# V's weights by contraction blocks in whole rows, and four V sums begun with two of five blocks

## The chip, the cores and the metric

The kernel runs on one core of one Trainium2 chip. The metric is the device time of one execution in microseconds; lower is better. The core has five instruction streams that run beside each other: TensorE (PE, with its weight loads shown as PEld), VectorE (DVE), ScalarE (ACT), GpSimd (POOL) and SyncE (SP). SP issues nearly all of the DMAs here.

## The reference, cut to what matters

The input x is 2048 rows of 640 columns in bf16. A layer norm of x goes into two branches, and their sum with x is the output: attention with 32 heads of 20 columns over a sliding window of 256 rows, and a gated feed-forward part with 1536 hidden columns.

```python
xn = _layernorm(x, axis=-1)                      # (1, 2048, 640)
qkv = xn @ wqkv                                  # wqkv: (640, 3 * 640), columns q | k | v
p = softmax(where(window of 256 keys back, q @ k.T * 20 ** -0.5, -1e9))
A = (p @ v) @ wo
B = (sigmoid(xn @ w_gate) * (xn @ w_up)) @ w_down
return x + A + B
```

## The kernel before

Rows are worked on in four chunks (`c`) of 512, and a chunk in four blocks (`s`) of 128 rows. The contraction over 640 columns is made of five blocks (`d`, `DC` = 5) of 128. `xnT[c]` holds the normed and transposed rows of a chunk, 128 partitions by five blocks by 512 rows; `wqkv` holds all of the q, k and v weights, 128 partitions by five blocks by 1920 columns, of which the last 640 are V's.

The order of every engine's instructions is the order in which the program writes them (`manual_schedule`). Chunk 0 is done by hand at the head; from then on a list of parts (`fill`) is pulled between the steps of the attention at build time, so that TensorE's order is fixed too.

**The head's loads.** SP issues, in this order: rows of x for blocks 0, 1 and 3 (`load_rows`, L157), V's weights for the columns of its first half (`load_v(0)`, L161: all five blocks, 320 columns), the rows of block 2, V's second half (`load_v(1)`), then the q and the k weights (`load_wqkv`, L151), and after those the gate and up weights (`load_gu`, L182).

**Norm and transposes.** Blocks 0 and 3 take their mean and variance on VectorE (`ln_half`, `ln_mv`), blocks 1 and 2 on ScalarE (`mean_act` L620, `root_act` L625 and L626); VectorE writes the normed rows `xn` for all of them (`norm` L273, `norm_act` L630 and L631). `transpose_rows(s, copy, lo, hi)` then turns the five 128 x 128 blocks of a row block on TensorE (`pt`, L280, in the PSUM pool `ps_h`, tag h), and the engine named by `copy` moves them to `xnT` (L281): ScalarE for block 0 in two parts, VectorE for the others.

**V's sums.** `project_v(c, s, hf)` makes one sum: the 128 rows of block `s` by the 320 columns of half `hf`, five matmuls of 128 x 320 (L329) into one PSUM bank `pv`. Eight of them stand in the head. A name such as v10 means block 1, half 0. `copy_v` evacuates a sum in two pieces of 64 rows (`us` 0 and 1) into the tile `v` (L338), by VectorE (`dve`) or ScalarE (`act`). PSUM has eight banks in the head: four under the tag d (pool `ps_d`) and four under the tag h (`ps_h`). A pool gives its banks in turn; two warming sums (`pwarm`, L233) take the first two of d. v30 and v31 stand in h, all other V sums in d.

TensorE's order in the head: the ten warming matmuls, the transposes of blocks 0 and 1, v00, v10, the transposes of block 3, v01, v30, v11, the transposes of block 2, v31, v20, v21, then the ten q and k sums (`proj_block`, L300), whose banks are d again. VectorE evacuates the q sums (L304), ScalarE the k sums (L306); they go by DRAM (`sq`, `sk`, L308) into the layout of the heads (`spread`, L318). After that come the gate and up sums (`pg` L414, `pu` L421) and the attention steps (`ps` L490, `acc` L523).

Of the kernel before, what the change touches and what calls it, by code (L numbers as in the profile page):

```python
# [9 lines left out]
P = 128  # L10
S = 2048
D = 640
# [3 lines left out]
DC = D // P  # L16
FC = F // P
CW = 512
# [4 lines left out]
GH = NG // 2  # L23
VW = DH + 1
VH = 16 * VW + 11
HALF = 320
FS = 768
EPS = 1e-5
# [10 lines left out]
FP32 = mybir.dt.float32  # L39
# [54 lines left out]
def kernel(  # L94
# [11 lines left out]
    nc = tc.nc  # L106
# [4 lines left out]
    def pool(name, bufs, **kw):  # L111
        return ctx.enter_context(tc.tile_pool(name=name, bufs=bufs, **kw))
# [15 lines left out]
    ps_d = pool("ps_d", 4, space=bass.MemoryType.PSUM)  # L128
# [13 lines left out]
    wqkv = const.tile([P, DC, 3 * D], BF16, name="wqkv")  # L142
    wqkv_r = A_wqkv.rearrange("(c p) n -> p c n", p=P)
# [6 lines left out]
    def load_wqkv(part):  # L150
        nc.sync.dma_start(out=wqkv[:, :, part * D:(part + 1) * D],  # L151
                          in_=wqkv_r[:, :, part * D:(part + 1) * D])
# [3 lines left out]
    def load_rows(s, queue):  # L156
        queue.dma_start(out=xc[0][:, s, :], in_=xr[:, s, :])  # L157

    def load_v(hf):
        a = 2 * D + hf * HALF  # L160
        nc.sync.dma_start(out=wqkv[:, :, a:a + HALF], in_=wqkv_r[:, :, a:a + HALF])  # L161

    load_rows(0, nc.sync)
    load_rows(1, nc.sync)
    load_rows(3, nc.sync)
    load_v(0)
    load_rows(2, nc.sync)
    load_v(1)
    load_wqkv(0)
    load_wqkv(1)  # L170

# [58 lines left out]
    for n in (6, 4):  # L230
        ps = ps_d.tile([P, CW], FP32, name="pwarm", tag="d")
# [18 lines left out]
    def ln_half(c, s, a, stats=None):  # L250
        if a == 0:
            stats = lnp.tile([P, 2, nc.vector.BN_STATS_DIM], FP32, name="stats")
        nc.vector.bn_stats(out=stats[:, a, :], in_=xc[c][:, s, a * HALF:(a + 1) * HALF])
        return stats
# [22 lines left out]
    def transpose_rows(s, copy, lo=0, hi=DC):  # L277
        pt = ps_h.tile([P, DC, P], BF16, name="pt", tag="h")
        for d in range(lo, hi):
            nc.tensor.transpose(pt[:, d, :], xns[0, s][:, d * P:(d + 1) * P], ident)  # L280
        copy(out=xnT[0][:, lo:hi, s * P:(s + 1) * P], in_=pt[:, lo:hi, :])  # L281
# [38 lines left out]
    def new_v(c, s):  # L320
        v = vp.tile([P, 2, VH], BF16, name="v")
        vt[c * SBC + s] = v
        nc.gpsimd.memset(v[:, :, 0:16 * VW].rearrange("p k (h d) -> p k h d", d=VW)[:, :, :, DH:VW], 0.5)
        nc.gpsimd.memset(v[:, :, 16 * VW:], 0.0)

    def project_v(c, s, hf, home=ps_d, tag="d"):
        ps = home.tile([P, CW], FP32, name="pv", tag=tag)
        for d in range(DC):
            nc.tensor.matmul(ps[:, 0:HALF], lhsT=xnT[c][:, d, s * P:(s + 1) * P],  # L329
                             rhs=wqkv[:, d, 2 * D + hf * HALF:2 * D + (hf + 1) * HALF],  # L330
                             start=(d == 0), stop=(d == DC - 1))
        return ps

    def copy_v(c, s, hf, ps, copy, us=(0, 1)):

        v = vt[c * SBC + s][hf * U:(hf + 1) * U, :, 0:16 * VW].rearrange("p k (h d) -> p k h d", d=VW)
        for u in us:
            copy(out=v[:, u, :, 0:DH],  # L338
                 in_=ps[u * U:(u + 1) * U, 0:HALF].rearrange("p (h d) -> p h d", d=DH))

    def proj_v(c, s, hf, copy):
        copy_v(c, s, hf, project_v(c, s, hf), copy)
# [265 lines left out]
    def root(mv):  # L608
        r = lnp.tile([P, 1], FP32, name="rstd")
        nc.scalar.activation(out=r, in_=mv[:, 1:2], func=SQRT, bias=eps)  # L610
        return r

    def norm(s, mv, r):
        nc.vector.reciprocal(r, r)
        norm_block(0, s, mv, r)
# [13 lines left out]
    def norm_act(s, xn, neg, r):  # L629
        nc.vector.reciprocal(r, r)  # L630
        nc.vector.tensor_scalar(out=xn, in0=xc[0][:, s, :], scalar1=neg[:, 0:1],  # L631
                                scalar2=r[:, 0:1], op0=ADD, op1=MULT)
        xns[0, s] = xn
# [4 lines left out]
    act, dve = nc.scalar.copy, nc.vector.tensor_copy  # L638
# [8 lines left out]
    norm_act(1, xn1, neg1, r1)  # L647
    mv3 = ln_mv(ln_half(0, 3, 1, stats3))
    transpose_rows(1, dve)
    v00 = project_v(0, 0, 0)  # L650
    r3 = root(mv3)
    xn2, neg2 = mean_act(2)
    r2 = root_act(2, xn2, neg2)
    norm(3, mv3, r3)
    v10 = project_v(0, 1, 0)
    copy_v(0, 0, 0, v00, dve, (0,))
    transpose_rows(3, dve)
    v01 = project_v(0, 0, 1)
    norm_act(2, xn2, neg2, r2)
    copy_v(0, 0, 0, v00, act, (1,))  # L660
    copy_v(0, 1, 0, v10, act)
    v30 = project_v(0, 3, 0, ps_h, "h")
    copy_v(0, 0, 1, v01, act)
    v11 = project_v(0, 1, 1)
    copy_v(0, 3, 0, v30, act)
    transpose_rows(2, dve)
    v31 = project_v(0, 3, 1, ps_h, "h")
    copy_v(0, 1, 1, v11, dve)
    copy_v(0, 3, 1, v31, act)
    proj_v(0, 2, 0, dve)  # L670
    proj_v(0, 2, 1, act)
# [75 lines left out]
    c = NCH - 1  # L747
# [62 lines left out]
```

## Time and profile before

| What | Value |
|---|---|
| Median of 3 timed runs | 309.93 us (309.67 to 310.23) |
| Profiled execution, its own time | 309.64 us |
| Its span, first to last instruction | 307.9 us |
| Granted TensorE clock | 1.000 |
| Busy of the span: PE, ACT, DVE, POOL | 98%, 64%, 56%, 55% |
| V matmuls of the head (L329) | 40, started from 7.0 to 13.1 us |
| First q matmul (L300) | 13.20 us |
| DMA in the first 13.2 us | 3.70 MB, mean 281 GB/s |

Times inside the profile are microseconds from the start of its span. A row of an order of time gives the start, the length, the engine, the line, what was written from what, and in brackets how long the engine had been idle and what released it. Matmuls overlap in their pipeline and their ends are modelled: the distance from start to start tells what one costs.

### The profile page before, as it was taken

How to read it: one execution, taken by the hardware profiler on the slowest of the kernel's cores; microseconds unless marked ns; L12 is line 12 of the kernel's file. 1: busy time of each engine (PE TensorE's matmuls, PEld its weight loads, DVE VectorE, ACT ScalarE, POOL GpSimd, SP SyncE). 2: the span in 40 equal slices, each digit the busy share in tenths (PEclk: the TensorE clock that was granted, in tenths of full speed). 3: DMA queues.
4: the chain of work that ended last, by engine and by line, in shares of the span. 5: the costliest groups of instructions: out<-in, count | busy, mean ns of one | idle time of the engine just before them, and what ended most of it. 6: DMA issues, size and time to landing. Idle time of an engine off the chain costs nothing.

```text
span 307.9 us, 9937 instructions
## 1 busy us (share of the span) xinstructions
PE 300.4 (98%) x4276; PEld 167.7 (54%) x4311; DVE 171.2 (56%) x339; ACT 198.4 (64%) x197; POOL 168.7 (55%) x308
## 2 busy tenths in 40 slices
PE   7999999999999999999999999999999999999995
PEld 3654444555657654554457654554546664444774
DVE  4633667648698364487946164383734536363523
ACT  6923877698854649888674547878585547688000
POOL 6000686687874828576672728457372937566000
PEclk9999999999999999999999999999999999999999
DMA  7997986984709363630015312650000200000202
GB/s 220 366 319 237 333 161 199 351 228 144 234 2 127 69 179 124 189 109 2 3 24 87 87 57 87 209 162 0 3 2 2 86 27 21 2 2 6 84 21 67
DMA packets 40460, 35.68 MB, mean 116 GB/s; under 512 B 10560, under 2 KB 39872, under 8 KB 40384
## 3 DMA queue, kind: packets, MB, share of 16 engines
q1 hardware_dynamic: 39552, 34.27, 38.6%
q10 hardware_dynamic: 864, 0.77, 0.8%
q8 instruction: 34, 0.56, 0.8%
q14 instruction: 10, 0.08, 0.1%
HBM read 23.63 MB, written 10.26 MB: 110 GB/s over the span
## 4 chain that ended last, share of the span: by engine, by line
PE 96%; issue 1%; DMA 1%; ACT 1%; DVE 0%; SPq 0%
PE y L435 18%; PE pu L421 17%; PE pg L414 17%; PE pqk L300 14%; PE ps L490 9%; PE pv L329 7%; PE y L442 7%; PE acc L523 6%; DMA xc<-in_A_x_dram 1%; PE pt L280 0%; ACT xn L620 0%; ACT xn L625 0%; DVE xn L631 0%; SPq L157 0%; ACT rstd L626 0%
## 5 line engine op out<-in xcount | busy, mean ns | idle before, releaser
L507 POOL TENSOR_SCALAR_AFFINE_SELECT pT<-pT 64x512 bf16<-64x512 bf16 (+1 forms) x256 | 157.1, 614 | 109.1 <-ACT pT L496 96.6
L496 ACT ACTIVATE pT<-ps 128x2048 bf16<-128x2048 f32 (+1 forms) x76 | 141.0, 1855 | 59.8 <-PE ps L490 57.9
L425 DVE SCALAR_TENSOR_TENSOR h<-th,pu 128x512 bf16<-128x512 f32 x48 | 32.8, 683 | 51.4 <-PE pu L421 44.9
L421 PE MATMUL pu<-xnT,wu 128*128 128x512 bf16 x228 | 59.0, 380 | 0.7 <-issue 0.2
L414 PE MATMUL pg<-xnT,wg 128*128 128x512 bf16 x226 | 58.5, 380 | 0.9 <-issue 0.3
L435 PE MATMUL y<-wd,h 128*128 128x320 bf16 (+2 forms) x396 | 56.8, 295 | 0.0
L300 PE MATMUL pqk<-xnT,wqkv 128*128 128x512 bf16 x191 | 45.4, 381 | 0.6 <-issue 0.2
L435 PEld LDWEIGHTS <-h 128*128 128x128 bf16 x396 | 36.7, 98 | 15.9 <-issue 1.8
L417 ACT ACTIVATE th<-pg 128x512 f32<-128x512 f32 x48 | 28.6, 595 | 15.5 <-PE pg L414 15.4
L414 PEld LDWEIGHTS <-wg 128*128 128x128 bf16 x240 | 22.3, 98 | 25.8 <-issue 2.0
L421 PEld LDWEIGHTS <-wu 128*128 128x128 bf16 x240 | 22.0, 98 | 25.5 <-issue 2.0
L300 PEld LDWEIGHTS <-wqkv 128*128 128x128 bf16 x200 | 22.5, 119 | 18.7 <-issue 1.4
L535 DVE STREAM_TRANSPOSE t<-acc 128x512 f32<-128x512 f32 x32 | 21.1, 696 | 20.1 <-PE acc L523 20.1
L490 PE MATMUL ps<-qT,kT 20*64 20x320 bf16 (+4 forms) x1440 | 32.1, 260 | 0.0
L490 PEld LDWEIGHTS <-kT 20*64 20x64 bf16 x1440 | 15.4, 103 | 24.9 <-issue 21.8
L446 DVE SCALAR_TENSOR_TENSOR rows<-y,rows 128x320 bf16<-128x320 f32 x30 | 14.4, 488 | 25.9 <-PE y L442 25.7
L547 DVE TENSOR_TENSOR on<-t,rec 128x320 bf16<-128x320 f32 (+4 forms) x48 | 27.8, 579 | 1.1
L329 PE MATMUL pv<-wqkv,xnT 128*128 128x320 bf16 x160 | 25.8, 300 | 0.0
L442 PE MATMUL y<-wo,oc 128*128 128x320 bf16 (+2 forms) x165 | 24.2, 295 | 0.0
L338 DVE CAST v<-pv 64x320 bf16<-64x320 f32 x29 | 14.1, 486 | 12.5 <-PE pv L329 12.3
L523 PE MATMUL acc<-pT,v 64*32 64x320 bf16 (+4 forms) x1440 | 19.7, 253 | 0.0
L523 PEld LDWEIGHTS <-v 64*32 64x32 bf16 x1440 | 16.2, 91 | 5.8 <-ACT pT L496 1.7
(48 smaller groups left out, 157.3 us busy)
## 6 DMA issues: line engine op xcount, KB each, us to landing
qT<-sq SPq DMA_DIRECT2D x16, 256.0 KB
kT<-sk SPq DMA_DIRECT2D x16, 256.0 KB
sq<-st SPq DMA_DIRECT2D x20, 128.0 KB
sk<-st SPq DMA_DIRECT2D x20, 128.0 KB
out_dram<-rows SPq DMA_DIRECT2D x15, 160.0 KB
wg<-in_B_w_gate_dram SPq DMA_DIRECT2D x4, 480.0 KB
wu<-in_B_w_up_dram SPq DMA_DIRECT2D x4, 480.0 KB
xc<-in_A_x_dram SPq DMA_DIRECT2D x3, 640.0 KB
```

Of the source, the lines that this page charges most:

```text
L300: nc.tensor.matmul(ps, lhsT=wt[:, m, :], rhs=xnT[c][:, d, :], start=(d == 0), stop=(d == DC - 1))
L329: nc.tensor.matmul(ps[:, 0:HALF], lhsT=xnT[c][:, d, s * P:(s + 1) * P], rhs=wqkv[:, d, 2 * D + hf * HALF:2 * D + (hf + 1) * HALF], start=( ...
L414: nc.tensor.matmul(pg, lhsT=part(wg, d, f), rhs=xnT[c][:, d, :], start=(d == 0), stop=(d == DC - 1))
L417: nc.scalar.activation(out=th, in_=pg, func=TANH, scale=0.5)
L421: nc.tensor.matmul(pu, lhsT=part(wu, d, f), rhs=xnT[c][:, d, :], start=(d == 0), stop=(d == DC - 1))
L425: nc.vector.scalar_tensor_tensor(out=h, in0=th, scalar=1.0, in1=pu, op0=ADD, op1=MULT)
L435: nc.tensor.matmul(y[:, 0:cut[1] - cut[0]], lhsT=ht[c, f][:, s * P:(s + 1) * P], rhs=wd[:, f, cut[0]:cut[1]], start=(f == 0), stop=False)
L442: nc.tensor.matmul(y[:, 0:cut[1] - cut[0]], lhsT=oc[c, m][:, s * P:(s + 1) * P], rhs=wo[:, m, cut[0]:cut[1]], start=False, stop=(m == DC - 1))
L490: nc.tensor.matmul(ps[a * U:(a + 1) * U, i, col * U:(col + n) * U], lhsT=qk["k", kc, o // GH][32 * i:32 * i + DH, o % GH + a, kb * U:(kb + ...
L496: nc.scalar.activation(out=pt[:, :, 0:width], in_=ps[:, :, 0:width], func=EXP, scale=SCALE)
L507: nc.gpsimd.affine_select(out=view, in_=view, pattern=[[0, HG], [0, n], [sign, U]], compare_op=GE, fill=0.0, base=base, channel_multiplier ...
L523: nc.tensor.matmul(acc[32 * i:32 * i + 32, q * U:(q + n) * U], lhsT=vt[kb][a * U:(a + 1) * U, u, h * VW:h * VW + 32], rhs=pt[a * U:(a + 1) ...
```

## The change

V's weights are still loaded in two DMAs in the same two places of SP's order, but cut along the contraction: first the blocks 0 and 1 with all 640 columns, then the blocks 2 to 4. A row of a packet is 1280 bytes instead of 640.

Four sums are split. v00 and v01 get their first two matmuls where v00 stood, v10 and v11 theirs where v10 stood. Then come the transposes of block 3, and after them the remaining three matmuls of v00, v01, v10 and v11. Then v30, the transposes of block 2, v31, v20 and v21, as before. `project_v` takes the range of blocks and an open bank for that.

The evacuations keep their engines, but are moved: on VectorE the first piece of v00 comes after the copy of xnT for block 3 instead of ahead of it, and the two pieces of v11 come ahead of the copy of xnT for block 2 instead of behind it. On ScalarE v01 is evacuated ahead of v10.

```diff
+VD = 2
...
-    def load_v(hf):
-        a = 2 * D + hf * HALF
-        nc.sync.dma_start(out=wqkv[:, :, a:a + HALF], in_=wqkv_r[:, :, a:a + HALF])
+    def load_v(lo, hi):
+        nc.sync.dma_start(out=wqkv[:, lo:hi, 2 * D:], in_=wqkv_r[:, lo:hi, 2 * D:])
...
-    load_v(0)
+    load_v(0, VD)
     load_rows(2, nc.sync)
-    load_v(1)
+    load_v(VD, DC)
...
-    def project_v(c, s, hf, home=ps_d, tag="d"):
-        ps = home.tile([P, CW], FP32, name="pv", tag=tag)
-        for d in range(DC):
+    def project_v(c, s, hf, home=ps_d, tag="d", lo=0, hi=DC, ps=None):
+        if ps is None:
+            ps = home.tile([P, CW], FP32, name="pv", tag=tag)
+        for d in range(lo, hi):
...
     transpose_rows(1, dve)
-    v00 = project_v(0, 0, 0)
+    v0 = [project_v(0, 0, hf, hi=VD) for hf in range(2)]
     r3 = root(mv3)
     xn2, neg2 = mean_act(2)
     r2 = root_act(2, xn2, neg2)
     norm(3, mv3, r3)
-    v10 = project_v(0, 1, 0)
-    copy_v(0, 0, 0, v00, dve, (0,))
+    v1 = [project_v(0, 1, hf, hi=VD) for hf in range(2)]
     transpose_rows(3, dve)
-    v01 = project_v(0, 0, 1)
+    for s, vs in enumerate((v0, v1)):
+        for hf in range(2):
+            project_v(0, s, hf, lo=VD, ps=vs[hf])
+    copy_v(0, 0, 0, v0[0], dve, (0,))
+    copy_v(0, 0, 0, v0[0], act, (1,))
+    copy_v(0, 0, 1, v0[1], act)
     norm_act(2, xn2, neg2, r2)
-    copy_v(0, 0, 0, v00, act, (1,))
-    copy_v(0, 1, 0, v10, act)
+    copy_v(0, 1, 0, v1[0], act)
+    copy_v(0, 1, 1, v1[1], dve)
     v30 = project_v(0, 3, 0, ps_h, "h")
-    copy_v(0, 0, 1, v01, act)
-    v11 = project_v(0, 1, 1)
+    transpose_rows(2, dve)
     copy_v(0, 3, 0, v30, act)
-    transpose_rows(2, dve)
     v31 = project_v(0, 3, 1, ps_h, "h")
-    copy_v(0, 1, 1, v11, dve)
     copy_v(0, 3, 1, v31, act)
     proj_v(0, 2, 0, dve)
     proj_v(0, 2, 1, act)
```

## The prediction

> **What bounds the kernel now.** I read the page first, then the busy time by stretches, then the chain of waits through the first 16 us, then TensorE's weight loads and VectorE's instructions in order of time, and last what the DMA engines moved. The page's engine line and its chain by engine come first.
>
> ```profile
> PE 300.4 (98%) x4276; PEld 167.7 (54%) x4311; DVE 171.2 (56%) x339; ACT 198.4 (64%) x197; POOL 168.7 (55%) x308
> ...
> PE 96%; issue 1%; DMA 1%; ACT 1%; DVE 0%; SPq 0%
> ```
>
> TensorE is busy 98% of the span and is 96% of the chain. The kernel's time is therefore the moment at which TensorE gets going plus everything it has to do, plus the few places where it waits. The stretches say where that could still be.
>
> ```profile
> 6.96:13.20 6.24, 6.24 (x54) 4.24 (x52) 4.58 (x13) 5.68 (x15) 0.00 (x0) 1.00 1.07 360
> 13.20:307.90 294.70, 288.83 (x4208) 161.39 (x4240) 163.56 (x319) 188.40 (x173) 163.82 (x286) 1.00 0.38 109
> ```
>
> The columns are the length, then busy time (and instructions) of PE, PE weight loads, DVE, ACT and POOL, the granted clock, the DMA share and GB/s. The first row is the V stage, which the change rewrites; at 13.20 the q projection (L300) begins. After 13.20 the order of TensorE's instructions is the same in both kernels, and in this trace TensorE's only idle entries there are some 0.7 us put down to issue. So I look for the new start of q: a shift of it goes through to the end one to one.
>
> ```profile
> 6.67 0.45 PE pt L280 x5
> 7.13 1.44 PE pv L329 x10
> 8.56 0.28 PE pt L280 x5
> 8.84 2.12 PE pv L329 x15
> 10.96 0.28 PE pt L280 x5
> 11.24 2.12 PE pv L329 x15
> ```
>
> This is the chain inside the V stage (start, length, what): TensorE alone, no DMA. V's weights are not what it waits for. By the landing records, the last piece of V's first column half arrives at 6.75 and of the second at 8.30; the first V matmul starts at 6.96, right behind the transposes of row block 1, and the first that needs the second half at 8.68. Modelled ends make PE look gapless here, so the real gaps must be read from the weight loads (start, length, idle before).
>
> ```profile
> 7.71 0.52 PEld L329 LDWEIGHTS <-xnT 128*128 128x128 bf16 x5 [0.24 <-DVE xnT L281]
> 8.32 0.35 PEld L280 LDWEIGHTS <-xn 128*128 128x128 bf16 x5
> ...
> 9.43 1.20 PEld L329 LDWEIGHTS <-xnT 128*128 128x128 bf16 x10 [0.24 <-DVE xnT L281]
> ...
> 11.82 1.20 PEld L329 LDWEIGHTS <-xnT 128*128 128x128 bf16 x10 [0.24 <-DVE xnT L281]
> ```
>
> Three times TensorE waits for VectorE's copy of a transposed block: for xnT of block 1, 3 and 2. V matmuls start 0.136 us apart and transposes 0.056, so five V matmuls begun at 6.96 are issued by 7.64 and the next starts at 7.71: 0.07 us lost, and 0.07 each at 9.43 and 11.82. The whole V stage loses 0.21 us. That is all that this profile lets a better order gain here.
>
> ```profile
> 8.19 0.48 DVE L338 CAST v<-pv 64x320 bf16<-64x320 f32 x1
> 8.88 0.49 DVE L281 COPY xnT<-pt 128x640 bf16<-128x640 bf16 x1 [0.22 <-PE pt L280]
> 9.62 0.16 DVE L630 RECIPROCAL rstd<-rstd 128x1 f32<-128x1 f32 x1 [0.25 <-ACT rstd L626]
> 9.82 0.45 DVE L631 TENSOR_SCALAR xn<-xc,neg,rstd 128x640 bf16<-128x640 bf16 x1
> 11.28 0.49 DVE L281 COPY xnT<-pt 128x640 bf16<-128x640 bf16 x1 [1.01 <-PE pt L280]
> 11.80 2.02 DVE L338 CAST v<-pv 64x320 bf16<-64x320 f32 x4
> ```
>
> VectorE in order. It stood idle 1.01 us before the copy of xnT for block 2, so that copy began as soon as the transposes were done. The two evacuations of v11 came after it, in the 2.02 us.
>
> **The change, part by part.** *The same work.* TensorE still runs 40 V matmuls and the same transposes, ACT still makes 11 V evacuations and DVE 5; POOL and SP keep their order. Only V's two DMA issues on SP differ in shape, 2 and 3 whole-row blocks for 5 half rows twice, 0.43 us of issue each now; nothing of the V stage waits for a later issue of SP. Cost nothing.
>
> *The loads.* V's 800 KB go in 640 packets of 1280 B for 1280 of 640 B. The trace has both sizes:
>
> ```profile
> 4.50:5.00 0.50, 0.50 (x2) 0.00 (x0) 0.16 (x1) 0.50 (x4) 0.45 (x2) 1.00 1.03 296
> 8.00:10.00 2.00, 2.00 (x20) 1.37 (x18) 1.50 (x5) 1.91 (x6) 0.00 (x0) 1.00 1.06 392
> ```
>
> In 4.50 to 5.00 only 640-byte packets ran (296 GB/s, median 32 ns each), in 8 to 10 only 1280-byte ones beside a few semaphore writes (392 GB/s, 55 ns). By packets the pair shortens by (1280 x 32 - 640 x 55) / 16 = 360 ns; by rates, 819 KB at 296 against 392 GB/s, by 0.68 us. So V is complete at about 7.6 to 7.9 where it was 8.30. The first piece falls from 410 KB to 328 KB, 0.28 us less at 296 GB/s, so 6.47 or earlier where it was 6.75. The needs are 6.96 and (below) 8.61: both hidden, with margins of 0.5 and 0.7 us. Bounds for each: 0 if so, and if the second lands with no gain at all, at 8.30, still 0. The Trainium skill's page "DMA: Bandwidth & Descriptors", section Specifications, puts line rate at 512 B and up, which would make both packet sizes equal and leave V complete at 8.30; the rows above (296 against 392 GB/s) disagree, and by the page's rule the sum stays the same with a margin of 0.3 us in place of 0.7. All later loads come forward by as much, and no matmul after 13.20 waits for one of them, so that gives nothing.
>
> *TensorE up to the third block.* v00 and v01 now take two matmuls each from 6.96: issued by 6.96 + 4 x 0.136 = 7.51. v10 and v11 need xnT of block 1, whose copy ends at 7.65 as before (its chain is untouched), and start at 7.71. The wait is 0.20 where it was 0.07: cost 0.13. Four matmuls end at 8.25. The transposes of block 3 need xn written at 8.27; a weight load followed such an end by 0.05 us at 7.71, 9.43 and 11.82, so they start at 8.33: a new wait of 0.07, which the fifth matmul of v10 covered before. They end at 8.61.
>
> *The rest of the four sums.* Twelve matmuls, 8.61 + 1.63 = 10.24. The wait of 0.07 for xnT of block 3 goes: VectorE makes that copy at about 8.82 to 9.31, straight behind the transposes, and v30 comes only at 10.24. After v30 (five matmuls, 10.92) the transposes of block 2 need xn2. VectorE now evacuates v00 first, from 9.33 to 9.82, so the reciprocal moves from 9.62 to 9.85 and xn2 from 10.27 to about 10.50. Cover 0.42 us; cost nothing. So far the change has lost 0.13 + 0.07 - 0.07 = 0.13 us.
>
> *The moved evacuation.* VectorE's queue now holds both evacuations of v11 ahead of the copy of xnT for block 2. v11's last matmul starts at 10.11 and the sum is readable some 0.32 later (10.66 to 10.98 in the trace), at 10.43; VectorE is free at 10.50, so 10.53 to 11.52 for two of 0.49. The transposes start at 10.92 and can be read at 11.38; the copy then runs 11.55 to 12.04 where it ran 11.28 to 11.77. TensorE finishes v31 at 10.92 + 0.28 + 0.68 = 11.88 and waits for that copy until 12.10: 0.22 in place of 0.07, cost 0.15. If VectorE got v11 0.2 us earlier this would be 0; if its row of three pieces ran 0.1 late, 0.25.
>
> *PSUM homes.* Four sums are open at once and fill all four banks of the d tag. v20 reuses v00's bank, read by 10.04 (ACT), v21 v01's, read by 10.9, the first q block v10's, read by 11.8, and they start at 12.1, 12.8 and 13.5. No wait. ACT's 11 evacuations end near 14.4 as now, and its next use is the k copy at 19.87.
>
> *Sum.* 0.13 + 0.15 = 0.28 on exact clocks 0.27: q starts at about 13.47 for 13.20, and the last instruction moves by as much. The profiled execution took 309.64 us (span 307.9), so it would take 309.91. The three timed runs have the median 309.93 (309.67 to 310.23), 0.29 above the profiled one; on them the forecast is 309.93 + 0.27 = 310.20, a loss of 0.09%. About 0.2%, 0.62 us, is what a measurement of this kernel can tell from no change, so I call it the same, on the slow side. Bounds of the unknown terms: +0.05 (no wait for the moved copy, the new gap at 8.25 closed) to +0.45.
>
> **The rivals.**
>
> *V's second piece decides (slower).* In the old order the second half was first used at 8.68 by one sum, with three more to follow much later; now all twelve middle matmuls, and with them v30 and the transposes of block 2, stand in one queue behind that load. If it lands after 8.61, each microsecond costs one. For it: one of the 16 DMA engines lagged the others by 0.6 us in both V loads (6.09 then 6.75; 7.67 then 8.30), and packets up to 0.77 us long ran near 3.8. Against it: the rates above. It shows as slower from a landing at 8.96; at 9.3 the time is 309.93 + 0.27 + 0.69 = 310.9. Chance 0.2.
>
> *V's first piece was late in ordinary executions (faster).* In the profiled one it was 0.21 us ahead of its use, but the timed median is 0.29 above that execution. If the whole 0.29 were waits for a first half that lands later, the smaller first piece would give it back: 309.93 + 0.27 - 0.29 = 309.9, the same. To be faster by 0.62 the usual wait would have to be 0.9 us, and the fastest timed run is only 0.26 below the median. Chance 0.08, nearly all as unknown variation.
>
> *The new waits do not form.* If VectorE takes v11 earlier than I work out, only the first gaps stay: 310.0. The same class; part of the 0.72.
>
> **How the numbers follow.** The forecast and its neighbours within 0.2% hold 0.72, the late second piece with other knock-on waits 0.20, faster 0.08. The low end, 309.5, is the best timed run less 0.2 (all three old gaps of 0.21 closed); the high end, 311.0, is the second rival value. The likeliest case alone spans 309.9 to 310.5.
>
> **What would show it.** Right: q's first matmul (L300) at about 13.45; weight loads of v10 still at 7.71, of block 3's transposes at 8.33, and of v20 at 12.1 behind VectorE's copy; V's two landings before 6.6 and 8.0; the stretch behind q's start 294.7 us long as now. Wrong: a V matmul that waits for a DMA near 8.6; q's start before 13.2; or a stretch behind q's start that differs by over 0.3 us, which would mean that something after the V stage moved that I took for fixed.

## The result, and the profile after

The changed kernel takes 311.02 us (median of 16 runs, 310.00 to 312.02) where the kernel before takes 309.92 (16 runs, 309.31 to 311.89): ratio 1.0033, 95% interval 1.0017 to 1.0048, a loss of 1.0 us by the ratio. The forecast was a loss of 0.27 us, called the same. The sign was right and the size was not: the median lies at the top end of the stated range (311.0), and the loss is clear of zero and, by its median, over the 0.2% bound. Its profiled execution took 310.83 us, with a span of 309.1 us against 307.9.

The chain by engine on the page after, and then the two stretches cut at the first V matmul and the first q matmul (columns as in the prediction):

```profile
PE 93%; DVE 2%; DMA 2%; issue 1%; SPq 1%; DVEq 0%
```

```profile
6.76:13.55 6.79, 6.55 (x54) 4.28 (x52) 4.68 (x13) 5.75 (x15) 0.00 (x0) 1.00 1.02 346
13.55:309.10 295.55, 288.87 (x4208) 161.32 (x4240) 163.93 (x319) 188.29 (x173) 163.49 (x286) 1.00 0.38 108
```

TensorE's share of the chain fell from 96% to 93%; VectorE (2%) and the DMA of V's weights (2%) are in it now. The V stage is 6.79 us long instead of 6.24, but began 0.20 earlier (6.76 for 6.96, because the rows of block 1 landed at 3.55 instead of 3.76 in this execution), so q starts at 13.55 instead of 13.20: 0.35 of the 1.2 us of span. The other 0.84 stands in the second row, 295.55 for 294.70, which the prediction took for fixed. That is over the 0.3 us that the prediction named as a sign of being wrong.

TensorE's weight loads in the V stage (start, length, idle before and its releaser):

```profile
7.50 0.39 PEld L330 LDWEIGHTS <-xnT 128*128 128x128 bf16 x4 [0.37 <-DVE xnT L281]
8.12 0.28 PEld L280 LDWEIGHTS <-xn 128*128 128x128 bf16 x5 [0.23 <-DVE xn L273]
...
8.78 2.13 PEld L330 LDWEIGHTS <-xnT 128*128 128x128 bf16 x16 [0.32 <-issue]
...
12.17 1.20 PEld L330 LDWEIGHTS <-xnT 128*128 128x128 bf16 x10 [0.31 <-DVE xnT L281]
```

The three waits of the prediction are there: for block 1's xnT (0.20 us by matmul starts), for block 3's xn (0.06) and for block 2's xnT (0.14). The fourth, ahead of 8.78, is not in its sum: the third matmul of v00 could have run at 8.41 and ran at 8.77. The records put the last landing of V's second piece at 8.73. This V matmul that waits for a DMA is another of the prediction's signs of being wrong. VectorE in order shows why the copy of block 2's xnT is later than before:

```profile
8.61 0.49 DVE L281 COPY xnT<-pt 128x640 bf16<-128x640 bf16 x1 [0.55 <-PE pt L280]
...
10.60 1.00 DVE L339 CAST v<-pv 64x320 bf16<-64x320 f32 x2 [0.19 <-PE pv L330]
11.63 0.49 DVE L281 COPY xnT<-pt 128x640 bf16<-128x640 bf16 x1
```

The two evacuations of v11 end at 11.60, and the copy follows them at once, as the prediction had it. Then the list of what TensorE waited for behind q's start has one row that the kernel before did not have (engine, line, releaser, total, times, longest):

```profile
PE y L436 <- DVE h L426: 0.8, 1, 0.8
```

It stands near 156 us, 140 us behind the code that was changed: the down projection of chunk 1 waits for the last `h`. VectorE there, first the kernel before, then the changed one:

```profile
150.78 0.32 DVE L547 TENSOR_TENSOR on<-t,rec 128x192 bf16<-128x192 f32 x1
...
153.20 1.30 DVE L273 TENSOR_SCALAR xn<-xc,mvs,rstds 128x640 bf16<-128x640 bf16 x2
154.42 0.67 DVE L425 SCALAR_TENSOR_TENSOR h<-th,pu 128x512 bf16<-128x512 f32 x1
```

```profile
151.15 0.82 DVE L548 TENSOR_TENSOR on<-t,rec 128x192 bf16<-128x192 f32 x1
...
154.07 1.50 DVE L273 TENSOR_SCALAR xn<-xc,mvs,rstds 128x640 bf16<-128x640 bf16 x2
155.50 0.67 DVE L426 SCALAR_TENSOR_TENSOR h<-th,pu 128x512 bf16<-128x512 f32 x1
```

The same multiply of 192 columns takes 0.82 us instead of 0.32. Everything behind it in VectorE's queue moves by that, and the two norm writes take 1.50 us instead of 1.30, which adds 0.20: `h` ends at 156.17, TensorE's next matmul starts at 156.22. In the kernel before `h` ended at 155.09 and TensorE took it 0.05 us later, so there was no slack at all: the 0.70 us by which VectorE fell back went through to TensorE. TensorE's weight loads for that matmul, first in the kernel before, then in the changed one:

```profile
155.14 0.79 PEld L435 LDWEIGHTS <-h 128*128 128x128 bf16 x7 [0.38 <-DVE h L425]
```

```profile
156.22 0.79 PEld L436 LDWEIGHTS <-h 128*128 128x128 bf16 x7 [1.08 <-DVE h L426]
```

### The profile page after: what moved, and what is told of

It reads as the page before. It is cut to its first block, busy times and chain, and to the rows that moved or that the text cites. A ratio compares the mean times of both kernels' runs of the same rounds, so it can differ in the third digit from the quotient of the medians.

```text
span 309.1 us, 9937 instructions
## 1 busy us (share of the span) xinstructions
PE 300.4 (97%) x4276; PEld 167.5 (54%) x4311; DVE 171.8 (56%) x339; ACT 198.4 (64%) x197; POOL 168.3 (54%) x308
## 4 chain that ended last, share of the span: by engine, by line
PE 93%; DVE 2%; DMA 2%; issue 1%; SPq 1%; DVEq 0%
PE y L436 17%; PE pu L422 16%; PE pg L415 16%; PE pqk L300 14%; PE ps L491 8%; PE y L443 7%; PE pv L330 7%; PE acc L524 6%; DMA wqkv<-in_A_wqkv_dram 2%; DVE on L548 1%; SPq L158 1%; DVE xn L273 0%; DVE h L426 0%; DVE oc L552 0%; SPq L161 0%
## 5 line engine op out<-in xcount | busy, mean ns | idle before, releaser
L508 POOL TENSOR_SCALAR_AFFINE_SELECT pT<-pT 64x512 bf16<-64x512 bf16 (+1 forms) x256 | 156.8, 612 | 110.5 <-ACT pT L497 98.0
L330 PEld LDWEIGHTS <-xnT 128*128 128x128 bf16 x160 | 14.7, 98 | 9.0 <-issue 1.1
```

What stands on the lines that cost most here:

```text
L508: nc.gpsimd.affine_select(out=view, in_=view, pattern=[[0, HG], [0, n], [sign, U]], compare_op=GE, fill=0.0, base=base, channel_multiplier ...
```

## The experiments

The twelve were timed in three groups of four (e1 to e4, e5 to e8, e9 to e12), the kernel before in each group with them: 310.25, 309.97 and 309.55 us. Medians of different groups are therefore compared by their ratios to it, and so are times that an expectation took from earlier runs.

**e1: the shift alone.** In the kernel before, ahead of the last V sum:

```diff
+        if (c, s, hf) == (0, 2, 1):
+            for _ in range(4):
+                nc.tensor.matmul(ps[:, HALF:CW], lhsT=xnT[c][:, 0, s * P:(s + 1) * P],
+                                 rhs=wqkv[:, 0, 2 * D:2 * D + CW - HALF], start=True, stop=True)
```

> The kernel before, with four extra matmuls of 192 columns on TensorE ahead of the last V sum (into columns of its bank that nobody reads). Nothing else changes: q starts 4 x 0.083 = 0.33 us later. Theory A (the shift of the head turns, near 155 us, VectorE's norm writes into GpSimd's selects, and TensorE waits for h): 309.92 + 0.33 + up to 0.73, about 310.6 to 311.0, with a wait of y for h near 155 in the profile. Theory B (the whole loss of 1.1 us is the head: V's second piece usually lands later than in the one profile): 310.25, no wait near 155 beyond what the kernel before has.

310.65 against 310.25, ratio 1.0016 (0.9998 to 1.0034). Against the kernel before, theory B asks for 0.33 us more and theory A for up to 1.06; the ratio gives 0.5, with an interval that holds both, so the median decides nothing. The profile does: it has the wait of y for h, 0.8 us, and the multiply at 151.47 with 0.82 us, with nothing of the change in the kernel. The late wait can come without the changed lines.

**e2: V's second piece ahead of the rows of block 2,** on the changed kernel:

```diff
     load_v(0, VD)
-    load_rows(2, nc.sync)
     load_v(VD, DC)
+    load_rows(2, nc.sync)
```

> The changed kernel, with V's second piece issued ahead of the rows of block 2. V is complete at about 8.73 - 160 KB / 390 GB/s = 8.3 or earlier, so TensorE's wait of 0.36 us for it goes. Theory B: the loss shrinks from 1.1 to about 0.3 us, 310.2. Theory A: the head gives back 0.36, the wait near 155 may stay: 310.3 to 310.7. Both: rows of block 2 land later, at about 7.7, which holds up ScalarE's mean of block 2 by 0.3 us, hidden ahead of the transposes at 11.

311.50, ratio 1.0038 (1.0025 to 1.0051): no gain, and my expectation of the cover was wrong. V was complete at 8.13 and TensorE no longer waited for it, but the rows of block 2 landed at 8.53 instead of 6.35, and ScalarE began their mean at 8.55 instead of 7.29. TensorE's weight loads show what that cost:

```profile
11.39 0.28 PEld L280 LDWEIGHTS <-xn 128*128 128x128 bf16 x5 [0.85 <-DVE xn L632]
...
12.94 0.11 PEld L330 LDWEIGHTS <-xnT 128*128 128x128 bf16 x2 [0.75 <-DVE xnT L281]
```

By matmul starts these are waits of 0.68 and 0.58 us. The chain mean, variance, norm of block 2 on ScalarE and VectorE had 0.66 us to spare in e3, where V came in time (the normed rows written at 10.03, their transposes at 10.69); here it fell back by 1.26. Block 2's rows can't give way to V's weights. This profile also has the late wait of y for h, 0.8 us.

**e3 and e4: the norm writes of chunk 3 behind the last h,** on the changed kernel (e3) and on the kernel before (e4). VectorE makes the four xn writes in one go after h instead of two ahead of it; TensorE's order stays.

```diff
-    def g_norms(c, turn):
+    def g_norms(c, turn, gap=3, each=True):
...
-        for _ in range(3):
+        for _ in range(gap):
             yield 0
...
             norm_block(c, s, mvs[:, s, :], rstds[:, s:s + 1])
-            yield 0
+            if each or s == SBC - 1:
+                yield 0
...
-    norms3 = g_norms(3, False)
+    norms3 = g_norms(3, False, 5, False)
```

> The changed kernel, with the four norm writes of chunk 3 on VectorE all put behind the last h of chunk 1, instead of two ahead of it and two behind. Theory A: the wait of y for h near 155 goes, 311.0 - 0.73 = 310.3. Theory B: nothing in the head moved, 311.0.

> The kernel before with the same edit. Its profile had a wait of 0.04 us at that place, so one execution would gain no more than that; if many of its executions also fall into the wait (they spread from 309.3 to 311.9), the median falls by up to 0.4. Theory A: 309.6 to 309.9, and the changed kernel with this edit stands 0.3 to 0.5 above it. Theory B: 309.9, and the distance of the two stays at 1.1.

e3: 309.82, ratio 0.9994 (0.9978 to 1.0009). e4: 309.62, ratio 0.9989 (0.9975 to 1.0004). Taking that one dependence out of TensorE's way takes the loss out of the changed kernel, as theory A said, though by more than its 0.73 us (ratio 1.0033 to 0.9994, 1.2 us); the two kernels then stand 0.20 us apart by medians, with overlapping intervals. In both profiles the stretch behind q's start is short again: 294.60 and 294.41 us. e4 also shows the kernel before in an execution in which V's first half came late, at 7.29 us:

```profile
7.33 1.18 PEld L329 LDWEIGHTS <-xnT 128*128 128x128 bf16 x9 [0.51 <-issue]
```

**e5 and e6: who comes first.** So far the multiply was 0.32 us in three profiles and 0.82 in three. At that moment GpSimd is in the third of four selects (L508) of the first step of chunk 2. Where the multiply was short, that select took 0.89 us; where it was long, 0.66. The third select, in the kernel before and in the changed one:

```profile
150.73 0.89 POOL L507 TENSOR_SCALAR_AFFINE_SELECT pT<-pT 64x512 bf16<-64x512 bf16 x1
```

```profile
151.10 0.66 POOL L508 TENSOR_SCALAR_AFFINE_SELECT pT<-pT 64x512 bf16<-64x512 bf16 x1
```

The two seem to exclude each other. e5 delays the select in the changed kernel, e6 the multiply in the kernel before (`tick` is a new tile of 128 x 4 that nobody reads):

```diff
 # e5, ahead of the third select
+            if (c, o) == (2, 0) and step is LATER[0] and sign < 0:
+                nc.gpsimd.memset(tick, 0.0)
 # e6, ahead of the multiply
+            if (c, g, slot) == (1, 6, 0):
+                nc.vector.memset(tick, 0.0)
```

> The changed kernel with one tiny GpSimd memset (128 x 4) ahead of the third select of the first step of chunk 2, which pushes that select some 0.1 us back. In the six profiles so far VectorE's multiply of 192 columns there starts 46 to 49 ns after that select; in three VectorE's multiply takes 0.32 us and the select 0.89, in three the select takes 0.66 and the multiply 0.82, and only then y waits 0.8 us for h. Theory C (a race for something the two engines share, which the changed kernel loses in most executions): VectorE now comes first always, multiply 0.32 us, no long wait of y, median 311.0 - 0.7 = 310.3. If the late h has another cause: 311.0.

> The kernel before with one tiny VectorE memset (128 x 4) ahead of that multiply of 192 columns, which pushes the multiply some 0.1 us back, so that GpSimd's select comes first always. Theory C: multiply 0.8 us, y waits 0.8 us for h near 155, median 310.6 to 310.9, with no execution left under 310.0. If the late h has another cause: 310.0 as before.

e5: 310.24, ratio 1.0011 (1.0000 to 1.0023), and no wait for h. e6: 310.29, ratio 1.0014 (1.0004 to 1.0024), a wait of y for h of 0.8 us, and a fastest execution of 309.99 where the kernel before had 309.28. So e5 took off 0.7 us by the ratios, as expected; e6 put on 0.4 and fell short of the 310.6 to 310.9 expected. GpSimd and then VectorE in e5, and VectorE in e6:

```profile
151.20 1.56 POOL L511 TENSOR_SCALAR_AFFINE_SELECT pT<-pT 64x512 bf16<-64x512 bf16 x2
```

```profile
151.06 0.32 DVE L551 TENSOR_TENSOR on<-t,rec 128x192 bf16<-128x192 f32 x1
```

```profile
150.67 0.81 DVE L550 TENSOR_TENSOR on<-t,rec 128x192 bf16<-128x192 f32 x1
```

With the select 0.15 us behind the multiply VectorE wins, with the multiply pushed 58 ns behind the select it loses, and the time follows. The Trainium skill, "SBUF — State Buffer", section "Who interferes with whom", says that VectorE and GpSimd share one pair of ports under an exclusive lock, that a VectorE instruction with two inputs in SBUF, as this multiply is, contends there with a GpSimd instruction that reads SBUF, and that issue order decides who blocks. The profiles agree: in all seven in which the multiply is long, it ends 0.21 us behind the end of the select, and in all seven in which it is short, the select ends 0.52 to 0.53 us behind the end of the multiply, although the starts lie from 150 ns one way to 61 ns the other way apart.

The price of a lost race can be read at the two y matmuls around that h, where the norm writes stand ahead of it: 0.34 to 0.35 us from start to start in the three profiles that won (before, e5, e11), 1.05 to 1.06 in the six that lost (after, e1, e2, e6, e9, e10). That is 0.71 us, the 0.50 of the multiply and the 0.20 of the norm writes.

**e7: the evacuations of v11 put back** behind the copy of xnT for block 2, on e3:

```diff
-    copy_v(0, 1, 1, v1[1], dve)
     v30 = project_v(0, 3, 0, ps_h, "h")
     transpose_rows(2, dve)
+    copy_v(0, 1, 1, v1[1], dve)
```

> The changed kernel with the norm writes of chunk 3 behind the last h (as in e3, where the race costs nothing) and with VectorE's two evacuations of v11 put back behind the copy of xnT for block 2. By the prediction's step on the moved evacuation: the wait ahead of v20 falls from 0.22 to 0.07 us, median 309.82 - 0.15 = 309.67; in the profile the gap ahead of v20 closes. If that step is wrong: 309.8.

309.66, ratio 0.9995 (0.9978 to 1.0013): the expected median, but e3 had the ratio 0.9994, so the times show no gain. The profile is sharper: the gap ahead of v20 closes from 0.14 us to 0.07. So the moved evacuation costs 0.07 us, half of the 0.15 of the prediction.

**e8: shift and norm writes together,** e1's edit on e4.

> The kernel before with the norm writes behind the last h (e4) and with the four extra matmuls of e1. With the wait for h out of the way a shift of the head of 0.33 us goes through one to one: 309.62 + 0.33 = 309.95. If a shift of the head sets off something else later: 310.3 or more.

309.65, ratio 0.9987 (0.9975 to 0.9999), below the expectation by 0.3 us, which is within the noise of the two runs; no sign that anything else is set off, but the shift itself, 0.32 us of head in the profile, isn't seen in the median either. Its profile is telling, because here VectorE lost the race:

```profile
150.94 0.82 DVE L552 TENSOR_TENSOR on<-t,rec 128x192 bf16<-128x192 f32 x1
...
153.29 1.25 DVE L430 SCALAR_TENSOR_TENSOR h<-th,pu 128x512 bf16<-128x512 f32 x2
```

Both h now stand right behind each other, the stretch behind q's start is 294.53, and TensorE waits for no h. In this profile the lost race costs nothing once two norm writes of 0.6 to 0.8 us each no longer stand ahead of h.

**e9, e10, e11: how often, and the head alone.** e9 is the changed kernel unaltered, e10 the changed kernel with e6's memset (meant to lose always), e11 the kernel before with e5's (meant to win always). In the one profile that each forced kernel has, the race went as meant.

> The changed kernel once more, unaltered. Theory C1 (its head makes it lose the race near 151 in most executions): median again about 311.0, most executions over 310.5, multiply of 0.82 us in the profile. Theory C2 (which side wins is luck of the hour or chip, and the head is the only lasting difference): median 310.2 to 310.7, spread over both groups.

> The changed kernel with the tiny VectorE memset of e6, so that it loses the race always. Theory C: 310.24 (e5, always won) + 0.7 = 310.9, that is the plain changed kernel's 311.0 if that one loses nearly always; against e6 (310.29) it shows the head alone: +0.2 to +0.5.

> The kernel before with the tiny GpSimd memset of e5, so that it wins the race always. Theory C: about 309.7, with the executions over 310.5 gone; against e5 (310.24) the head alone: changed minus before +0.2 to +0.5.

e9: 310.97, ratio 1.0037 (1.0019 to 1.0054); in its profile the multiply takes 0.82, y waits 0.8 us for h, and V's second piece comes at 8.96:

```profile
9.00 0.50 PEld L330 LDWEIGHTS <-xnT 128*128 128x128 bf16 x4 [0.28 <-issue]
```

e11: 309.48, ratio 0.9996 (0.9983 to 1.0009), with no execution over 310.25. e10: 311.59 (8 runs), ratio 1.0052 (1.0033 to 1.0070), higher than expected. Its profile is its fastest execution (310.47, V in time, the race lost), so nothing recorded shows what took another microsecond in the others. With the race won, the changed kernel stands at 1.0011 (e5) against 0.9996 (e11) for the kernel before, 0.5 us apart; with the race lost, at 1.0052 (e10) against 1.0014 (e6), 1.2 us apart. Each of these distances is uncertain by some 0.6 us, but the second is more than the head's 0.2 us: the race is not all that parts the two kernels.

**e12: the cut after three blocks,** `VD = 3` on e7.

> A try at a faster version: e7 (norm writes behind the last h, evacuations of v11 put back) with the cut of V's weights after three blocks instead of two. Six matmuls of v00 and v01 (0.82 us) cover the wait for xnT of block 1 and the wait for the transposes of block 3 goes too: 0.20 + 0.07 us less, 309.66 - 0.27 = 309.4, if the first piece, now 480 KB, lands by 6.8; in the profiles 320 KB landed at 5.93 to 6.86 and 400 KB at 6.58 to 7.29, so a wait of up to 0.6 can take it all back: 309.4 to 310.0.

309.52, ratio 1.0001 (0.9983 to 1.0020). In the profile the gaps went as worked out: the V stage has one wait left, and q starts at 12.89, with the first piece landed at 6.70.

```profile
11.52 1.20 PEld L330 LDWEIGHTS <-xnT 128*128 128x128 bf16 x10 [0.24 <-DVE xnT L281]
```

That profiled execution took 308.98 us, but the median shows no gain over the kernel before. e3, e4, e7, e8, e11 and e12 all beat the changed kernel by their medians; none is shown to beat the kernel before by an amount worth having.

## Why the prediction was right or wrong

**The gaps (0.13 + 0.07 - 0.07): right.** The wait for block 1's xnT is 0.20 us and for block 3's transposes 0.06, the wait ahead of v30 is gone.

**The moved evacuation (0.15): mis-sized.** It is 0.07: TensorE waits 0.14 us ahead of v20 instead of 0.22. I had VectorE still busy with xn2 when v11 was ready, 0.07 us too long; in e3 it was done with xn2 at 10.03, and the evacuations began with v11 itself at 10.21, so the copy came that much earlier. The sum of the head without loads is 0.20 instead of 0.27: q minus the start of block 1's transposes is 6.53 us in the kernel before and 6.72 in e3.

**The loads: wrong for the second piece.** I put V's completion at 7.6 to 7.9 from the packet rates. The six profiles of kernels with this cut and this order of loads have 7.94, 8.07, 8.40, 8.48, 8.73 and 8.96. Rates set the bulk, but some of the 16 DMA engines trail: in the profile after fifteen had finished at 7.60 and the last came at 8.73; in e9 twelve had finished at 7.49 and the last four came from 8.26 to 8.96. TensorE started behind the last one (8.77 and 9.00). I had seen the lag of 0.6 us in the trace of before and named it under the first rival, without putting it into the margin. The first rival is real, with no wait in three of the six profiles and 0.14, 0.32 and 0.36 us in the others, not its full price.

**The first piece: the second rival is real too.** In six profiles with the old cut the first half landed at 6.58 to 7.29, and TensorE waited for it, up to 0.55 us, in four of them, the profile of before being one of the two with none. With the new cut it landed at 5.71 to 6.40 in six profiles, with no wait, and at 6.86 in e2, with one of 0.15. The change does what its shape says for the first piece and gives it back at the second.

**"A shift of it goes through to the end one to one": the step that failed.** Of the 1.2 us of span, 0.84 are behind q's start, 0.70 of them ahead of one h and the rest not traced. My reason was a list in which TensorE's matmuls wait for nothing but issue. A matmul that is modelled to be still running hides the wait in front of the next one; the list of weight loads had a wait of 0.4 us for this h, and the two y matmuls there start 0.34 us apart where 0.136 is usual. So the kernel before already waited 0.2 us at that place, and VectorE's queue, with a race against GpSimd in it, stood on the path. A lost race costs 0.71 us there, and that is where most of the loss is: e3 takes all of the loss away, e5 takes 0.7 of the 1.0 us away by the race alone, e6 puts 0.4 us into the kernel before. The prediction had no term for it, so that the sign came out right is in this part luck, and the top of the range, which stood for a late second piece, was reached mostly by another way.

**What stays open.** Why the changed kernel loses the race more often. In ten profiles without a forced outcome VectorE won five and lost five, with the multiply recorded 46 to 47 ns behind the select in wins and 47 to 49 in losses; the changed kernel unaltered lost in both of its profiles, and 14 of its 16 and 9 of its 12 timed executions are over 310.5, as against 21 of the 117 of the kernel before. That line doesn't part won from lost, though: e6, which lost, has 3 of 12 over it, and e5, which won, 3 of 12 too. What speaks for it more is that forcing a win gained the changed kernel 0.7 us and the kernel before nothing clear (e11). Its shift alone (e1) and a shift with the norm edit (e8) lost as well. That a later head tips it is suggested, not shown: e3, e7 and e12 have the changed head too, and won. Nor is there a run whose memset leaves the order as it was, to show that the memset alone costs nothing. And e10's extra microsecond has no profile.

## What to carry to other kernels

A margin is judged against the last of a DMA's engines and not against the queue's rate, and an engine that is "98% busy" still has places without slack: look for weight loads and start distances that wait, since modelled ends hide them. Before a shift is called one to one, find the places further on where the critical engine takes its operand the moment it is made, and ask which other engines share a resource with its maker there. Taking such a dependence out of the way (e3) was worth as much as the whole loss here, with no change to the stage that was at issue.

## What the runs showed of the hardware that I had not expected

The conflict between VectorE and GpSimd did not show as idle time: it lengthened the loser's own record (0.32 to 0.82 us for the multiply, 0.66 to 0.89 for the select). The order of recorded starts does not name the winner either: the select is recorded first in all ten undisturbed profiles, by 46 to 49 ns, and half of them went to the multiply. The Trainium skill's page "SBUF — State Buffer", section "Who interferes with whom" ("Issue order, not op shape, decides who blocks."), fits e5, where the starts are 0.15 us apart; at under 0.05 us the trace can't tell who issued first.
